# Linear attention feeding a GELU feed-forward block: k and v laid out nine tokens to a partition, numerators in four 64x64 tiles of TensorE

## The chip, the cores and the metric

The kernel runs on one core of one Trainium2 chip. The metric is the device time of one execution in microseconds (us); each time given is a median of several executions. Engines are named as the profile names them: PE is TensorE's matmul stream and PEld its weight loads, DVE is VectorE, ACT is ScalarE, POOL is GpSimd, SP is SyncE, whose queue issues the loads and the DMA transposes.

## The reference, cut to what matters

For each of 8 batches and 8 heads, with 576 tokens of 64 elements, a linear attention is computed, and its result goes through a feed-forward block with a tanh GELU.

```python
phi = lambda x: np.where(x > 0, x, np.exp(x) - 1.0) + 1.0
q_p, k_p = phi(q), phi(k)                        # (8, 8, 576, 64)
kv  = np.einsum('bhsd,bhse->bhde', k_p, v)       # 64 x 64 for each head
z   = np.sum(k_p, axis=2)
num = np.einsum('bhsd,bhde->bhse', q_p, kv)
den = np.einsum('bhsd,bhd->bhs', q_p, z)[..., None] + 1e-06
x   = (num / den).transpose(0, 2, 1, 3).reshape(4608, 512)
h   = x @ w_in                                   # 512 -> 2048
out = gelu_tanh(h) @ w_out                       # 2048 -> 512
```

The sum over tokens in kv does not care which token lies on which partition, so k and v may be laid out in any way that both share. The order of q's tokens decides the rows of the output.

## The kernel before: the parts that matter

The kernel treats 512 tokens of each batch as one group (four chunks of 128 tokens), and the last 64 tokens of all batches, two batches side by side, as a ninth group. `iteration(j)` runs the feed-forward block of group j in 32 slots: 16 of `h` (four matmuls each, then a GELU on ACT) and 16 of `o` (four matmuls each). Work for the next batches is put between slots by `at(j, slot, ...)`; `run` executes it after the slot's matmuls.

```python
def h_mm(h_ps, xt, m, ts=slice(0, MAIN)):          # one slot of h: 4 matmuls of 128x512
    for c in range(KM):
        nc.tensor.matmul(h_ps[:, ts], lhsT=w_in_sb[:, c, P*m : P*(m+1)], rhs=xt[:, c, ts], ...)
```

In batches 0 and 1, k and v lie nine tokens to a partition (one partition holds a run of nine tokens of one head, a partition half for each of two heads of a pair), and kv is made by 72 matmuls in 64x64 tiles. From batch 2 on, k and v lie four tokens to a partition for 512 tokens, and the last 64 come in separate tiles (`kr`, `vr`) shared by two batches, with the other batch's half of `vr` zero; kv is made by 40 matmuls that use 128 rows and 64 columns of the array.

```python
def kv_paired(b, ii, kv_of):                       # batches 0 and 1: 64x64 tiles
    for j in range(J):                             # J = 9
        for s in range(2):
            for a in range(2):
                r, u = slice(HP*a, HP*(a+1)), 2*ii + s
                nc.tensor.matmul(kv_of(a, ii)[HP*s : HP*(s+1)],
                                 lhsT=kp[r, j, u, :], rhs=vp[r, j, u, :], ...)

def kv_main(b, i, kv_ps):                          # batches 2 to 7: 128x64 tiles
    for c in range(C + 1):                         # 4 chunks and the rest
        for s in range(2):
            h = 2*i + s
            nc.tensor.matmul(kv_ps[HP*s : HP*(s+1), i, :],
                             lhsT=kp[:, c, h, :] if c < C else kr[:, 0, h, :],
                             rhs=vp[:, c, h, :] if c < C else vr[:, h, :], ...)
```

The numerator and denominator of a chunk come from four matmuls, one for each pair of heads, against a block-diagonal 128x130 tile `kvbd` (the off-diagonal blocks are zero; the 65th column of a block is z). DVE divides.

```python
def nab_mm(qt_c, kvbd, ns, rows=slice(0, P)):
    for i in range(NP):                            # NP = 4 pairs of heads
        nc.tensor.matmul(ns[i//2][rows, 2*E*(i%2) : 2*E*(i%2+1)],
                         lhsT=qt_c[:, i, rows], rhs=kvbd[:, i, :], ...)   # E = 65
...
def nab_evac(n_ps, paired):
    nc.vector.reciprocal(r, n_v[:, :, :, D])
    nc.vector.tensor_tensor(x_view(x, paired), n_v[:, :, :, 0:D], r[...].to_broadcast(...), op=ALU.mult)
```

The schedule of the later batches:

```python
def plan_prepare(b, s_linear, s_exp):
    ...
    at(j, s, linear, "q"); at(j, s + 1, linear, "k"); at(j, s + 2, casts)
    j, s = s_exp
    at(j, s, exps_all)          # q, then k, then kr
    at(j, s + 2, least_q)       # phi of q, and its four DMA transposes to qt
    at(j, s + 4, least_k)

def plan_attention(b, j, s_kv, s_n):
    ...
    at(j, s_kv, kv)
    for c in range(C):
        at(j, s_n[c], n, c)     # nab, then a DMA transpose of x to xt
...
for b in range(4, B):
    plan_prepare(b, (b - 2, 13), (b - 2, 15))
    if b > 4:
        at(b - 3, 23, load_batch, b)
for m in range(1, 4):
    at(2*m - 1, 18, load_rest, "qr", q, m)
    plan_rest(m, 2*m, 15, 22, (4, 5, 7)[m - 1])
for b in range(3, B):
    plan_attention(b, b - 1, 2, (4, 6, 8, 10))
```

PSUM's eight banks are six of a rotating pool (`bank`: h, o, kv, and n where it is made in single banks) and one pair (`pair_of_banks`) for n.

Of the kernel before, what the change touches and what calls it, by code (L numbers as in the profile page):

```python
# [15 lines left out]
def kernel(  # L16
# [34 lines left out]
    prest = ctx.enter_context(tc.tile_pool(name="prest", bufs=1))  # L51
# [31 lines left out]
    PAIRED = (0, 1)  # L83

    def ld_tile(name, b):
        shape = [P, NP, J * D] if b in PAIRED and name != "q" else [P, H, C * D]
        ld[name, b] = pld.tile(shape, FP32, name=name + "_x", tag="ld")
# [10 lines left out]
    def load_main(name, src, b):  # L98
        ld_tile(name, b)
        nc.sync.dma_start(  # L100
            out=ld[name, b],
            in_=src[b, :, 0:MAIN, :].rearrange("h (p c) d -> p h (c d)", c=C),
        )

    def load_rest(name, src, m):
        t = (pqr if name == "qr" else prest).tile([P, H, D], FP32, name=name)
        ld[name, m] = t
        for s in range(2):
            r = t[REST * s : REST * (s + 1)]
            rows = src[2 * m + s, :, MAIN:S, :]  # L110
            if name == "qr" and m == 0:
                for a in range(2):
                    nc.sync.dma_start(
                        out=r[:, NP * a : NP * (a + 1), :],
                        in_=rows.rearrange("(u a) p d -> p a u d", a=2)[:, a],
                    )
            else:
                nc.sync.dma_start(out=r, in_=rows.rearrange("h p d -> p h d"))

    def load_batch(b):  # L120
        load_main("q", q, b)
        load_main("k", k, b)
        if b % 2 == 0:
            load_rest("kr", k, b // 2)
            load_rest("vr", v, b // 2)
        load_main("v", v, b)
# [43 lines left out]
    load_main("q", q, 3)  # L170
    load_main("k", k, 3)
# [8 lines left out]
    vrs = [const.tile([P, H, E], BF16, name=f"vr{s}") for s in range(2)]  # L180
    kvbds = [const.tile([P, NP, 2 * E], BF16, name=f"kvbd{i}") for i in range(4)]
    for i in range(2):
        nc.gpsimd.memset(vps[i][:, :, D:E], 1.0)
        nc.gpsimd.memset(kvbds[i], 0.0)
    for s in range(2):
        nc.gpsimd.memset(kvbds[2 + s], 0.0)
        nc.gpsimd.memset(vrs[s], 0.0)
        nc.gpsimd.memset(vrs[s][REST * s : REST * (s + 1), :, D:E], 1.0)
# [3 lines left out]

    def vp_main(b):
        return vps[b % 2][:, 0 : C * H].rearrange("p (c h) e -> p c h e", h=H)
# [5 lines left out]
    def by_chunk(t, hs):  # L200
        return t[:, :, hs, :].rearrange("p c h d -> p h c d")
# [5 lines left out]
    def exp_of(name, b, hs=None):  # L207
        x = ld[name, b]
        hs = hs or slice(0, x.shape[1])
        if (name, b) not in exps:  # L210
            exps[name, b] = pe.tile([P, x.shape[2] // D, x.shape[1], D], BF16, name=name + "_e")
        nc.scalar.activation(  # L212
            by_chunk(exps[name, b], hs),
            x[:, hs].rearrange("p h (c d) -> p h c d", d=D),
            AF.Exp,
        )

    def linear_of(name, b, hs=None):
        x = ld[name, b]
        hs = hs or slice(0, x.shape[1])  # L220
        if (name, b) not in phi:
            phi_tiles(name, b)
        nc.vector.tensor_scalar(  # L223
            by_chunk(phi[name, b], hs),
            x[:, hs].rearrange("p h (c d) -> p h c d", d=D),
            1.0,
            1.0,
            op0=ALU.add,
            op1=ALU.max,
        )  # L230
# [14 lines left out]

    def cast_v(b, fn):
        fn(
            out=vp_main(b)[:, :, :, 0:D].rearrange("p c h d -> p h c d"),
            in_=ld["v", b].rearrange("p h (c d) -> p h c d", d=D),
        )  # L250

    def cast_vr(m):
        for s in range(2):
            r = slice(REST * s, REST * (s + 1))
            nc.vector.tensor_copy(out=vrs[s][r, :, 0:D], in_=ld["vr", m][r])
# [16 lines left out]
    def kv_main(b, i, kv_ps):  # L272
        kp, vp = phi["k", b], vp_main(b)
        kr, vr = phi["kr", b // 2], vrs[b % 2]
        for c in range(C + 1):
            for s in range(2):
                h = 2 * i + s
                nc.tensor.matmul(  # L278
                    kv_ps[HP * s : HP * (s + 1), i, :],
                    lhsT=kp[:, c, h, :] if c < C else kr[:, 0, h, :],  # L280
                    rhs=vp[:, c, h, :] if c < C else vr[:, h, :],
                    start=(c == 0),
                    stop=(c == C),
                    skip_group_check=True,
                )

    def kv_evac(b, blocks, src, fn):
        for s in range(2):
            r = slice(HP * s, HP * (s + 1))
            fn(out=kvbds[b % 4][r, blocks, E * s : E * (s + 1)], in_=src[r])  # L290

    def nab_mm(qt_c, kvbd, ns, rows=slice(0, P)):
        for i in range(NP):
            nc.tensor.matmul(  # L294
                ns[i // 2][rows, 2 * E * (i % 2) : 2 * E * (i % 2 + 1)],
                lhsT=qt_c[:, i, rows],
# [4 lines left out]
    def x_view(x, paired):  # L301
        return x.rearrange("p (u a d) -> p a u d" if paired else "p (a u d) -> p a u d", a=2, d=D)

    def nab_evac(n_ps, paired):
        n_v = n_ps[:, :, 0 : 4 * E].rearrange("p a (u e) -> p a u e", e=E)
        r = psm.tile([P, 2, NP], FP32, name="r")
        nc.vector.reciprocal(r, n_v[:, :, :, D])  # L307
        x = px.tile([P, d_model], BF16, name="x")
        nc.vector.tensor_tensor(  # L309
            x_view(x, paired),  # L310
            n_v[:, :, :, 0:D],
            r[:, :, :, None].to_broadcast([P, 2, NP, D]),
            op=ALU.mult,
        )
        return x

    def nab(qt_c, b):
        n_ps = pair_of_banks("n_ps")
        nab_mm(qt_c, kvbds[b % 4], [n_ps[:, a] for a in range(2)])
        return nab_evac(n_ps, b in PAIRED)  # L320

    def nab_in_banks(qt_c, b):
        ns = [bank("n_ps", [P, 4 * E]) for _ in range(2)]
        nab_mm(qt_c, kvbds[b % 4], ns)
        x = px.tile([P, d_model], BF16, name="x")
        for a in range(2):
            n_v = ns[a].rearrange("p (u e) -> p u e", e=E)
            r = psm.tile([P, NP], FP32, name="r1")
            nc.vector.reciprocal(r, n_v[:, :, D])
            nc.vector.tensor_tensor(  # L330
                x_view(x, b in PAIRED)[:, a],
                n_v[:, :, 0:D],
                r[:, :, None].to_broadcast([P, NP, D]),
                op=ALU.mult,
            )
        return x
# [184 lines left out]
    def plan_prepare(b, s_linear, s_exp):  # L521
        rest = b % 2 == 0

        def linear(n):
            linear_of(n, b)
            if rest and n == "k":
                linear_of("kr", b // 2)

        def casts():
            cast_v(b, nc.vector.tensor_copy)  # L530
            if rest:
                cast_vr(b // 2)

        def exps_all():
            for n in "qk":
                exp_of(n, b)
            if rest:
                exp_of("kr", b // 2)

        def least_q():  # L540
            least_of("q", b)
            qts[b] = pt.tile([P, C, NP, P], BF16, name="qt")
            for c in range(C):
                nc.sync.dma_start_transpose(
                    out=qts[b][:, c],
                    in_=phi["q", b][:, c].rearrange("p h d -> p (h d)"),
                )

        def least_k():
            least_of("k", b)  # L550
            if rest:
                least_of("kr", b // 2)

        j, s = s_linear
        at(j, s, linear, "q")
        at(j, s + 1, linear, "k")
# [3 lines left out]
        at(j, s + 2, least_q)  # L560
        at(j, s + 4, least_k)

    def plan_attention(b, j, s_kv, s_n):
        def kv():
            if j == 1:
                kv_ps = pair_of_banks("kv_ps")[:, 0, 0 : NP * E].rearrange("p (i e) -> p i e", e=E)
            else:
                kv_ps = bank("kv_ps", [P, NP, E])
            for i in range(NP):
                kv_main(b, i, kv_ps)  # L570
            kv_evac(b, slice(0, NP), kv_ps, nc.vector.tensor_copy)

        def n(c):
            x = nab(qts[b][:, c], b)
            if c == 0:
                xts[b] = pt.tile([P, NP, MAIN], BF16, name="xt")
            nc.sync.dma_start_transpose(out=xt_chunk(b, c), in_=x)

        at(j, s_kv, kv)
        for c in range(C):  # L580
            at(j, s_n[c], n, c)

    def plan_rest(m, j, s_exp, s_least, j_n):
        box = {}

        def least():
            linear_of("qr", m)
            least_of("qr", m)
            box["qt"] = psm.tile([P, NP, P], BF16, name="qtr")
# [164 lines left out]
```

## Time and profile before

| | |
|---|---|
| time | 287.52 us, median of 3 (287.31 to 287.77) |
| profiled span | 285.5 us, TensorE clock granted 0.998 |
| PE busy | 278.1 us (97%), 1864 matmuls |
| PEld busy | 136.5 us (48%) |
| ACT busy | 163.8 us (57%) |
| DVE busy | 107.7 us (38%) |
| POOL busy | 20.5 us (7%) |
| DMA | 53.76 MB, mean 188 GB/s |

Busy time of an engine is the time in which one of its instructions ran, and shares are of the span. Matmuls overlap in their pipeline, so PE's busy time says that it always had one under way, not that each ran at its best spacing; what a group of matmuls costs is read from when the next group starts. The chain of waits follows the work back from the last instruction, and what stands in it set the end.

### The profile page before, as it was taken

Reading aid. Unit: us, or ns where it says so; the run is one execution under the profiler, and the core shown is the slowest. Engines: PE = TensorE matmul, PEld = TensorE weight load, DVE = VectorE, ACT = ScalarE, POOL = GpSimd, SP = SyncE. Lnnn points to the kernel's source line nnn. Section 1 sums busy time; section 2 is a strip of 40 time slices with the busy share of each in tenths; the row PEclk is TensorE's granted clock in tenths of the full one; section 3 lists DMA queues with packets and bytes.
Section 4 is the critical chain, followed back from the end, with each engine's and each line's share of the span. In section 5 each row is a group of like instructions: output and inputs, shape, how many; then the busy total and the mean of one; then the engine's idle time right before and its main releaser. Section 6 shows DMA issues by size and latency. Waiting matters only on the chain.

```text
span 285.5 us, 4570 instructions
## 1 busy us (share of the span) xinstructions
PE 278.1 (97%) x1864; PEld 136.5 (48%) x1864; DVE 107.7 (38%) x182; ACT 163.8 (57%) x226; POOL 20.5 (7%) x26
## 2 busy tenths in 40 slices
PE   8789999999999999999999999999999999999995
PEld 3464455445454445544554455444544444444444
DVE  3840468534855473543246614640412010000001
ACT  4866865795966935683458635763572275027400
POOL 6066250000000000000000000000000000000000
PEclk9999999999999999999999999999999999999999
DMA  7999999966979948936899489435141230120022
GB/s 247 410 406 397 410 400 270 365 229 195 146 231 327 252 141 230 340 75 149 227 276 216 115 219 363 79 103 156 37 39 45 87 53 0 53 86 10 0 74 74
DMA packets 71539, 53.76 MB, mean 188 GB/s; under 512 B 42080, under 2 KB 62944, under 8 KB 71520
## 3 DMA queue, kind: packets, MB, share of 16 engines
q1 hardware_dynamic: 68736, 44.58, 55.8%
q10 hardware_dynamic: 2784, 8.91, 8.7%
q8 instruction: 14, 0.23, 0.3%
q14 instruction: 5, 0.04, 0.0%
HBM read 36.70 MB, written 9.44 MB: 162 GB/s over the span
## 4 chain that ended last, share of the span: by engine, by line
PE 93%; DMA 3%; DVE 1%; SPq 1%; issue 0%; ACTq 0%; ACT 0%; DVEq 0%
PE h_ps L349 44%; PE o_ps L650 43%; PE n_ps L294 3%; DMA v_x<-in_v_dram 3%; PE kv_ps L278 1%; PE t_ps L341 1%; SPq L91 1%; PE kv_ps L263 0%; SPq L96 0%; PE t_ps L474 0%; DVE x L330 0%; DVE vp L241 0%; DVE x L309 0%; PE w_ps L385 0%; ACTq L616 0%
## 5 line engine op out<-in xcount | busy, mean ns | idle before, releaser
L650 PE MATMUL o_ps<-w_out_sb,g 128*128 128x512 bf16 (+2 forms) x608 | 127.5, 368 | 0.0
L349 PE MATMUL h_ps<-xt,w_in_sb 128*128 128x512 bf16 (+1 forms) x552 | 117.6, 363 | 0.0
L359 ACT ACTIVATE g<-h_ps 128x512 bf16<-128x512 f32 x144 | 85.0, 598 | 46.2 <-PE h_ps L349 45.2
L650 PEld LDWEIGHTS <-g 128*128 128x128 bf16 x608 | 57.8, 98 | 64.4
L349 PEld LDWEIGHTS <-w_in_sb 128*128 128x128 bf16 x616 | 56.4, 97 | 59.7 <-issue 0.6
L611 ACT COPY o_sb<-o_ps 128x512 f32<-128x512 f32 (+2 forms) x20 | 11.1, 561 | 60.6 <-PE o_ps L650 53.5
L611 DVE COPY o_sb<-o_ps 128x512 f32<-128x512 f32 (+1 forms) x18 | 12.0, 666 | 69.9 <-PE o_ps L650 69.9
L307 DVE RECIPROCAL r<-n_ps 128x8 f32<-128x8 f32 x33 | 6.8, 207 | 49.0 <-PE n_ps L294 48.9
L309 DVE TENSOR_TENSOR x<-n_ps,r 128x512 bf16<-128x512 f32 x33 | 22.8, 691 | 1.1
L212 ACT ACTIVATE q_e<-q_x 128x2048 bf16<-128x2048 f32 (+1 forms) x9 | 15.5, 1721 | 2.8 <-DMA q_x<-in_q_dram 2.7
L212 ACT ACTIVATE k_e<-k_x 128x2048 bf16<-128x2048 f32 (+2 forms) x9 | 15.8, 1755 | 0.8 <-DMA k_x<-in_k_dram 0.8
L223 DVE TENSOR_SCALAR q_p<-q_x 128x2048 bf16<-128x2048 f32 (+1 forms) x9 | 9.9, 1100 | 14.2 <-DMA q_x<-in_q_dram 14.2
L236 DVE TENSOR_TENSOR q_p<-q_p,q_e 128x2048 bf16<-128x2048 bf16 (+1 forms) x9 | 9.9, 1105 | 13.4 <-ACT q_e L212 13.3
L349 PE MATMUL h_ps<-xt_rest,w_in_sb 128*128 128x512 bf16 x64 | 14.0, 379 | 0.0
L294 PEld LDWEIGHTS <-qt 128*128 128x128 bf16 x128 | 9.7, 98 | 6.9 <-DVE x L309 0.4
L294 PE MATMUL n_ps<-kvbd,qt 128*128 128x130 bf16 x128 | 12.5, 221 | 0.0
L223 DVE TENSOR_SCALAR k_p<-k_x 128x2048 bf16<-128x2048 f32 (+2 forms) x9 | 10.2, 1132 | 5.4 <-DMA k_x<-in_k_dram 5.4
L236 DVE TENSOR_TENSOR k_p<-k_p,k_e 128x2048 bf16<-128x2048 bf16 (+2 forms) x9 | 11.0, 1227 | 0.8 <-ACT k_e L212 0.7
L290 DVE CAST kvbd<-kv_ps 64x260 bf16<-64x260 f32 (+2 forms) x18 | 6.6, 365 | 10.7 <-PE kv_ps L278 8.2
L385 PE MATMUL w_ps<-warm 128*128 128x512 bf16 x32 | 9.3, 444 | 1.2 <-DVE warm L177 1.2
L376 ACT ACT_TABLE_LOAD x8 | 10.3, 1283 | 0.1
L212 ACT ACT_TABLE_LOAD x8 | 10.3, 1283 | 0.1
(49 smaller groups left out, 96.6 us busy)
## 6 DMA issues: line engine op xcount, KB each, us to landing
out_dram<-o_sb ACTq DMA_DIRECT2D x16, 512.0 KB, 3.1
q_x<-in_q_dram SPq DMA_DIRECT2D x6, 1024.0 KB, 7.5
k_x<-in_k_dram SPq DMA_DIRECT2D x6, 1024.0 KB, 11.3
v_x<-in_v_dram SPq DMA_DIRECT2D x6, 1024.0 KB, 7.5
w_st<-in_moe_w_in_dram SPq DMA_DIRECT2D x4, 1024.0 KB, 14.5
w_st<-in_moe_w_out_dram SPq DMA_DIRECT2D x4, 1024.0 KB, 13.6
q_x<-in_q_dram SPq DMA_DIRECT2D x4, 512.0 KB, 8.5
k_x<-in_k_dram SPq DMA_DIRECT2D x2, 576.0 KB, 5.6
```

The costliest lines, as they stand in the source:

```text
L212: nc.scalar.activation(by_chunk(exps[name, b], hs), x[:, hs].rearrange("p h (c d) -> p h c d", d=D), AF.Exp,)
L223: nc.vector.tensor_scalar(by_chunk(phi[name, b], hs), x[:, hs].rearrange("p h (c d) -> p h c d", d=D), 1.0, 1.0, op0=ALU.add, op1=ALU.max,)
L236: nc.vector.tensor_tensor(p, p, e, op=ALU.min)
L294: nc.tensor.matmul(ns[i // 2][rows, 2 * E * (i % 2) : 2 * E * (i % 2 + 1)], lhsT=qt_c[:, i, rows], rhs=kvbd[:, i, :], skip_group_check=True,)
L307: nc.vector.reciprocal(r, n_v[:, :, :, D])
L309: nc.vector.tensor_tensor(x_view(x, paired), n_v[:, :, :, 0:D], r[:, :, :, None].to_broadcast([P, 2, NP, D]), op=ALU.mult,)
L349: nc.tensor.matmul(h_ps[:, ts], lhsT=w_in_sb[:, c, P * m : P * (m + 1)], rhs=xt[:, c, ts], start=(c == 0), stop=(c == KM - 1), skip_group_ ...
L359: nc.scalar.activation(g[:, m, :], h_ps, AF.Gelu_apprx_tanh)
L376: nc.scalar.preload_act_table_set("gelu_apprx_tanh_and_others")
L385: nc.tensor.matmul(w_ps, lhsT=warm[:, 0:P], rhs=warm)
L611: (nc.scalar.copy if on_scalar else nc.vector.tensor_copy)(dst, src)
L650: nc.tensor.matmul(o_ps, lhsT=g[:, m, P * t : P * (t + 1)], rhs=w_out_sb[:, m, fs], start=(m == 0), stop=(m == MM - 1),)
```

## The change

It makes one form out of two. In all batches k and v come in nine tokens to a partition, so the separate tiles for the last 64 tokens of k and v, their loads, their maps and the zeroed `vr` tiles go. The numerators of batches 3 to 7, and of all leftover tokens of q, are made in four 64x64 tiles of the array from a plain `kv` tile (128x65 for a pair of heads) instead of the block-diagonal one. Two chunks are made in one slot, at two slots of a group (5 and 21) instead of four (4, 6, 8, 10) and one for kv (2); the next batch's kv shares the later slot. Loads of batches 5 to 7 are issued at slot 6 of a group instead of 23. In batches 4 to 7 the map of k runs ahead of that of q. The aim is to enter the small-tile modes of TensorE less often and to use all of the array in them.

The core of the diff, with cuts:

```diff
-    def load_main(name, src, b):
+    def load_q(b):
+        ...
+    def load_all_pairs(name, src, b):
         ld_tile(name, b)
-        nc.sync.dma_start(
-            out=ld[name, b],
-            in_=src[b, :, 0:MAIN, :].rearrange("h (p c) d -> p h (c d)", c=C),
-        )
+        load_pairs(name, src, b)
...
-    def kv_main(b, i, kv_ps):
-        ...
+    def kv_of_head(b, s, i):
+        r = slice(HP * s, HP * (s + 1))
+        return kvs[b % 4][r, i, :] if b > 2 else kvbds[b][r, i, E * s : E * (s + 1)]
+
+    def n_quads(qt_c, bs, ns):
+        for i in range(NP):
+            for t in range(2):
+                for s in range(2):
+                    c = slice(HP * t, HP * (t + 1))
+                    nc.tensor.matmul(
+                        ns[s][c, E * i : E * (i + 1)],
+                        lhsT=qt_c[HP * s : HP * (s + 1), i, c],
+                        rhs=kv_of_head(bs[t], s, i),
+                        skip_group_check=True,
+                    )
...
+        order = "qk" if b < 4 else "kq"
...
-        at(j, s + 2, least_q)
-        at(j, s + 4, least_k)
+        if b < 4:
+            at(j, s + 2, least_q, b)
+            at(j, s + 4, least_of, "k", b)
+        else:
+            at(j, s + 2, least_of, "k", b)
...
+    def plan_attention(b, m_rest):
+        j = b - 1
+        def pair_of_chunks(c):
+            in_banks = nab_quads_in_banks(qts[b][:, c + 1], (b, b))
+            in_pair = nab_quads(qts[b][:, c], (b, b))
+            return (c + 1, in_banks), (c, in_pair)
+        def early():
+            chunks = pair_of_chunks(0)
+            if m_rest is not None:
+                rest = nab_quads_in_banks(rest_qt[m], (2 * m, 2 * m + 1))
+            ...
+        def late():
+            chunks = pair_of_chunks(2)
+            if b + 1 < B:
+                kv_ps = [bank("kv_ps", [P, 2, E]) for _ in range(2)]
+                for ii in range(2):
+                    kv_paired(b + 1, ii, lambda a, ii: kv_ps[a][:, ii, :])
+            for c, x_of in chunks:
+                transposed_x(b, c, x_of())
+            if b + 1 < B:
+                ...                                # kv copied to SBUF on DVE
+                least_q(b + 1)
+        at(j, 5, early)
+        at(j, 21, late)
...
-    plan_attention(2, 1, 16, (18, 20, 22, 24))
+    plan_third()                                   # kv_in_pair(2) at (1, 16), four n as before
...
+    at(2, 2, kv_in_pair, 3)
     for b in range(4, B):
         plan_prepare(b, (b - 2, 13), (b - 2, 15))
-        if b > 4:
-            at(b - 3, 23, load_batch, b)
...
-    for b in range(3, B):
-        plan_attention(b, b - 1, 2, (4, 6, 8, 10))
+    for b in range(3, B):
+        plan_attention(b, {4: 0, 5: 1, 6: 2, 7: 3}.get(b))
+    for b in range(5, B):
+        at(b - 3, 6, load_batch, b)
```

Batches 0 and 1 keep their code. Batch 2 keeps the block-diagonal numerators, with its kv now made by the 72 matmuls of `kv_paired`.

## The prediction, made before the changed kernel ran

> **What bounds the kernel now.** I read the busy shares first, then the chain of waits, then the chain in order of time, because only the last says what a small group of matmuls costs. The page's first and fourth parts:
>
> ```profile
> PE 278.1 (97%) x1864; PEld 136.5 (48%) x1864; DVE 107.7 (38%) x182; ACT 163.8 (57%) x226; POOL 20.5 (7%) x26
> ...
> PE 93%; DMA 3%; DVE 1%; SPq 1%; issue 0%; ACTq 0%; ACT 0%; DVEq 0%
> ```
>
> PE is the bound. The chain leaves PE only in the first 16 us and in the last microsecond; the 3% of DMA is the first loads, which the change keeps. So only time taken out of PE's stream after 60 us counts. The chain in order of time (start, length, what, number of matmuls), first in batch 1, then around two later groups:
>
> ```profile
> 41.45 0.71 PE kv_ps L263 x72
> 42.16 0.97 PE o_ps L650 x4
> ...
> 43.60 0.86 PE o_ps L650 x4
> ...
> 80.92 0.76 PE kv_ps L278 x40
> 81.68 1.83 PE h_ps L349 x8
> 83.51 0.23 PE n_ps L294 x4
> 83.74 1.73 PE h_ps L349 x8
> ...
> 110.34 0.37 PE n_ps L294 x8
> 110.71 0.64 PE kv_ps L278 x40
> 111.35 1.83 PE h_ps L349 x8
> 113.18 0.23 PE n_ps L294 x4
> 113.41 1.73 PE h_ps L349 x8
> ```
>
> The reader is to see two things. Eight full matmuls take 1.73 us (216 ns each), but 1.83 us after a kv, so leaving a small-tile mode costs 0.1 us that the chain books on the matmuls behind. And nothing stands between the pieces: in steady groups PE waits for nobody. The extra time of a group over its 128 full matmuls is therefore the sum of its small pieces.
>
> [...] Read record by record, the first small-tile matmul starts 93 ns later than a full one would have, and the first full one starts about 125 ns after the last small one and is followed by one spaced 10 ns too wide. [...]
>
> **The change, part by part.** First the unit costs, all from the trace before.
>
> - A chunk of numerators, 4 matmuls of 128x130: 0.236 us from where the next full matmul could have started, without a mode change.
> - kv in 40 matmuls of 128x64: 0.76 + 0.10 = 0.86 us. With the 8 leftover numerators ahead in the same mode: 0.37 + 0.64 + 0.10 = 1.11 us. The last leftovers alone (group 7): 0.46 + 0.01 = 0.47 us.
> - kv in 72 matmuls of 64x64, that is 18 rounds of four tiles: 0.71 + (0.97 - 0.86) = 0.82 us. Its rounds start on average 33 ns apart (0.563 us from the first to the eighteenth), so an episode of R rounds costs about 0.22 + 0.033 R us. This is an estimate from one episode. The 0.22 is entering and leaving.
>
> A chunk in 64x64 tiles is 16 matmuls, 4 rounds. So, after the change, two chunks alone are 8 rounds, 0.48 us; two chunks and the leftovers 12 rounds, 0.62 us; two chunks and a kv 26 rounds, 1.08 us.
>
> | group j | before | after |
> |---|---|---|
> | 1 (batch 2) | 0.86 + 4 x 0.236 = 1.80 | 0.82 + 0.94 = 1.76 |
> | 2 | 1.80 | kv of batch 3 alone 0.82, early 0.48, late 1.08 = 2.38 |
> | 3, 4, 5 | 1.11 + 0.94 = 2.05 each | 0.62 + 1.08 = 1.70 each |
> | 6 | 1.80 | 0.62 + 0.48 = 1.10 |
> | 7 | 0.47 | 0 |
> | sum | 12.0 | 10.3 |
>
> The sum is **1.7 us less**. It is a small number because the numerators of one chunk fall only from 0.236 to 0.13 us, kv is hardly cheaper in 72 small matmuls than in 40 larger ones, and each group of batches 3 to 6 now pays for a small-tile mode twice where it paid once. Group 2 gets slower because it carries two kv.
>
> Now what moves off PE, and whether it comes back as a wait. The late slot's kv needs the map of k of the same group. I place it on the trace before, group 5's start of o at 153.28:
>
> ```profile
> 153.93 1.28 ACT L212 ACT_TABLE_LOAD   x1
> 154.90 1.23 DVE L247 CAST vp<-v_x 128x2048 bf16<-128x2048 f32 x1 [2.37 <-DMA v_x<-in_v_dram]
> 155.23 1.91 ACT L212 ACTIVATE q_e<-q_x 128x2048 bf16<-128x2048 f32 x1
> ...
> 157.17 1.23 DVE L236 TENSOR_TENSOR q_p<-q_p,q_e 128x2048 bf16<-128x2048 bf16 x1 [0.25 <-ACT q_e L212]
> ```
>
> After the change k goes first, with 2304 elements to a partition: its exp takes 2.11 us (batch 1's row of that shape), so 155.23 to 157.34, and the minimum on DVE 1.23 x 2304/2048 = 1.38 us, to 158.75. PE reaches slot 21's end at 153.28 + 6 x 0.864 = 158.46, enters the mode (0.09), does 8 rounds (0.27) and wants k at 158.82. That is 0.07 us of slack: none, within my error. I charge an expected wait of 0.06 us in four groups, **0.25 us**.
>
> The other deadlines have room. DVE, free at 158.75, copies one output tile (0.69), divides two chunks (1.3 in single banks, 0.9 in the pair) and is done at 161.7; the two DMA transposes need some 1.4 us of SP each and land 2.6 to 3.7 us after issue, so by about 166, while the next group starts at 153.28 + 13.82 + 1.08 = 168.2. The transposes of the next q follow, by about 171, and are wanted at slot 5 of the next group, 173.4. PSUM: with the leftovers, the early slot takes four extra banks of six; the GELU of slot 3 must be done by the end of slot 5, and GELUs run about 0.9 us behind their matmuls, so it is.
>
> Off PE, DVE gains about 0.37 us for each pair of chunks and each leftover tile divided in single banks (two reciprocals and two multiplies, 1.27, against 0.90), loses the maps of kr and the casts of vr (0.42 + 0.42 + 0.87 in three batches); ACT loses three exps of 0.61 us and gains 0.2 us for each k. All of it is beside PE. The loads lose 12 transfers of 128 KB in 256-byte rows, and come earlier; the one visible DMA wait there, the 2.37 us ahead of the v cast, ends no wait of PE.
>
> 287.52 - 1.74 + 0.25 = **286.0 us**.
>
> **The rivals.** (1) *kv waits for k in the late slot.* The slack above is nil. If ACT or DVE runs 0.4 us later than I placed them, four groups lose 0.4 us each, the gain is gone, and the time is about 287.4. The order k before q speaks for an author who saw that wait and cured it. (2) *The new numerators run slower than batch 1's kv.* They load a new weight tile for every 65 columns, as kv does, but a late slot holds 104 matmuls in a row where the trace shows 72 at most, and in the last rounds of those 72 the starts within a round already spread from 3 to 8 ns. At 60 ns a round instead of 33, the 96 rounds of numerators (20 chunks and 4 leftover tiles, 4 rounds each) would cost 2.6 us more: about 288.6. (3) *The transposes land late*, since two chunks now come only 10 slots before the next group; it would show as a wait of h at a group's head, at most 1 us in five groups, 289 or more. The margin of 2 us speaks against it. (4) *The gain is larger*, since earlier and longer loads help: nothing in the steady chain waits for a load, so I give this nothing beyond 0.3 us.
>
> **Range and chances.** The account gives 285.8 without any wait and 287.4 if rival 1 is full; numerators at 27 ns a round (65 columns at the rate of 216 ns for 512) would take 0.6 us off the former, 285.2. I take 285.2 to 287.1 for 8 in 10. A gain of over 2% needs 5.75 us, nearly half of all small pieces (12 us): 1 in 100. Over 2% slower needs a stall of more than 1 us in most groups: 2 in 100.
>
> **What would show each step.** In the chain of the changed kernel: late pieces of about 0.97 us for x104 followed by 0.11 us more on the next four matmuls; early pieces of 0.37 to 0.5 us; a period of 29.3 us in groups 3 to 5 (27.64 + 1.70) against 29.67 now; group 2 longer by 0.6 us; group 7 at 27.6 us. A wait of PE's kv for DVE's k minimum is rival 1; wider rounds without a wait are rival 2; a wait of h for a DMA at a group's head is rival 3. I am wrong if tiles that do not accumulate behave differently from batch 1's, or if DVE reaches its deadlines later than placed.

## The result, and the profile after

The changed kernel takes **297.0 us** (median of 6, 295.58 to 298.27), against 287.56 for the kernel before beside it: 1.0327 times as long, with a 95% interval of 1.0288 to 1.0366. I had predicted 286.0, with 287.1 as the upper end. The profiled run of the changed kernel is the longest of its six, with a span of 296.5 us against 285.5.

The busy shares and the chain by engine, first and fourth parts of its page:

```profile
PE 280.2 (95%) x2294; PEld 137.1 (46%) x2328; DVE 105.0 (35%) x197; ACT 161.2 (54%) x221; POOL 17.9 (6%) x21
...
PE 82%; DMA 11%; DVE 3%; issue 2%; SPq 1%; ACT 0%; ACTq 0%; DVEq 0%
```

PE's busy time hardly moved (278.1 to 280.2), which by itself would say that nothing had happened. The chain says otherwise: DMA had 3% of it, all in the first microseconds, and now has 11%. The waits of PE (who waits, for whom, us in total, times, longest) name two that were not there. Before, all of them; then the first three after:

```profile
PE kv_ps L263 <- DVE vp L241: 1.5, 2, 1.1
PE w_ps L385 <- DVE warm L177: 1.2, 1, 1.2
PE t_ps L341 <- DVE x L309: 0.8, 1, 0.8
PE t_ps L341 <- DVE x L330: 0.5, 1, 0.5
```
```profile
PE h_ps L348 <- DMA xt<-x: 4.4, 2, 3.6
PE kv_ps L236 <- DVE vp L225: 1.9, 2, 1.2
PE kv_ps L236 <- DVE k_p L220: 1.4, 1, 1.4
```

Of the three, the middle one belongs to the first two batches, whose code did not change (1.5 us before); the first and the last are new. The chain in order of time (start, length, what) shows them in place:

```profile
88.30 0.38 PE n_ps L270 x32
88.68 1.85 PE h_ps L348 x4
...
91.09 10.61 DMA v_x<-in_v_dram
...
103.00 1.36 DVE k_p L220
...
104.41 0.78 PE kv_ps L236 x72
...
105.34 2.05 PE o_ps L672 x9
107.39 9.98 DMA xt<-x
...
117.50 4.42 PE h_ps L348 x10
```

In group 2 the late slot's kv of batch 4 starts at 104.41, late because DVE's minimum for k stands behind the cast of v, and v lands at 101.70. Then a transpose of x issued at 107.39 takes 9.98 us to land, and h of group 3 starts at 117.50. Its first ten matmuls take 4.42 us; at full clock ten take 2.16. PE had idled 3.6 us, and its matmuls run at half clock until 123.5, for 6 us. SyncE's queue shows what was issued ahead of that transpose, batch 5's three loads:

```profile
98.36 0.54 SPq L98 DMA_DIRECT2D q_x<-in_q_dram  x1
99.02 2.53 SPq L89 DMA_DIRECT2D k_x<-in_k_dram  x1
101.66 0.45 SPq L89 DMA_DIRECT2D v_x<-in_v_dram  x1
106.08 5.15 SPq L569 DMA_TRANSPOSE xt<-x  x2
```

The last of these loads lands at 115.0, the two transposes at 116.6 and 117.4.

The loss of 11.0 us in span, read from the starts of the groups in both chains:

| stretch | lost in it |
|---|---|
| until group 1 begins (48.5 us before, 51.6 after) | 3.1 |
| group 1 and the wait at the head of group 2 (78.25, 82.08) | 0.7 |
| group 2 and the wait at the head of group 3 (107.75, 117.50) | 5.9 |
| group 3, in its beginning at half clock | 2.8 |
| groups 4 to 8 | -1.5 |

The first row is the surprise: the code and the transfers of that stretch are unchanged. The windows of both profiles (stretch, length, busy time of each engine, granted clock, DMA share, GB/s) show slower transfers. Before, then after:

```profile
0.00:40.00 40.00, 36.06 (x307) 19.37 (x308) 18.96 (x33) 29.27 (x38) 18.26 (x25) 1.00 0.99 378
```
```profile
0.00:40.00 40.00, 35.34 (x277) 19.71 (x281) 16.48 (x31) 26.41 (x35) 14.88 (x19) 0.91 0.99 357
```

The DMA engines are full in both (0.99), but move 357 GB/s instead of 378. Read packet by packet between 5 and 40 us, the 2048-byte packets have a median of 87 ns instead of 84, those of 2304 bytes 98 instead of 93. The clock of 0.91 is something else: one fall to half, from 14.2 to 21.1 us, after a stretch (10 to 14 us) in which PE was busy for 2.01 of 4 us. Two of the later profiles have this fall too, and o of their first group starts at 33.7 to 34.0 us; six others with equally slow loads do not have it, and there o starts at 31.4 to 31.8.

### The profile page after: what moved, and what is told of

The parts are those of the page before. It is cut to its first block, busy times and chain, and to the rows that moved or that the text cites. A ratio compares the mean times of both kernels' runs of the same rounds, so it can differ in the third digit from the quotient of the medians.

```text
span 296.5 us, 5430 instructions
## 1 busy us (share of the span) xinstructions
PE 280.2 (95%) x2294; PEld 137.1 (46%) x2328; DVE 105.0 (35%) x197; ACT 161.2 (54%) x221; POOL 17.9 (6%) x21
## 4 chain that ended last, share of the span: by engine, by line
PE 82%; DMA 11%; DVE 3%; issue 2%; SPq 1%; ACT 0%; ACTq 0%; DVEq 0%
PE h_ps L348 41%; PE o_ps L672 35%; DMA v_x<-in_v_dram 7%; DMA xt<-x 4%; PE kv_ps L236 2%; PE n_ps L270 1%; PE n_ps L252 1%; PE t_ps L340 1%; DVE x L283 1%; SPq L89 1%; DVE k_p L220 0%; DVE q_p L214 0%; DVE q_p L220 0%; SPq L94 0%; PE t_ps L473 0%
## 5 line engine op out<-in xcount | busy, mean ns | idle before, releaser
L348 PE MATMUL h_ps<-xt,w_in_sb 128*128 128x512 bf16 (+2 forms) x537 | 117.3, 373 | 5.4 <-DMA xt<-x 4.4
L348 PEld LDWEIGHTS <-w_in_sb 128*128 128x128 bf16 x616 | 59.2, 101 | 71.2 <-issue 9.4
L283 DVE TENSOR_TENSOR x<-n_ps,r 128x256 bf16<-128x256 f32 (+1 forms) x53 | 27.6, 520 | 1.8
L282 DVE RECIPROCAL r<-n_ps 128x4 f32<-128x4 f32 (+1 forms) x53 | 9.8, 184 | 49.1 <-PE n_ps L270 43.2
L220 DVE TENSOR_TENSOR k_p<-k_p,k_e 128x2304 bf16<-128x2304 bf16 (+1 forms) x9 | 11.0, 1223 | 20.1 <-ACT k_e L206 20.1
L206 ACT ACTIVATE k_e<-k_x 128x2304 bf16<-128x2304 f32 (+1 forms) x9 | 17.1, 1905 | 1.0 <-DMA k_x<-in_k_dram 0.9
L214 DVE TENSOR_SCALAR k_p<-k_x 128x2304 bf16<-128x2304 f32 (+1 forms) x9 | 11.0, 1220 | 12.5 <-DMA k_x<-in_k_dram 12.5
L225 DVE CAST vp<-v_x 128x2304 bf16<-128x2304 f32 (+1 forms) x9 | 10.4, 1159 | 0.9 <-DMA v_x<-in_v_dram 0.9
L236 PE MATMUL kv_ps<-vp,k_p 64*64 64x65 bf16 x576 | 6.5, 194 | 3.3 <-DVE vp L225 1.9
L129 POOL CAST w_in_sb<-w_st 128x2048 bf16<-128x2048 f32 (+1 forms) x5 | 7.7, 1551 | 16.1 <-DMA w_st<-in_moe_w_in_dram 16.1
```

Of the source, the lines that this page charges most:

```text
L206: nc.scalar.activation(o, i, AF.Exp)
L214: nc.vector.tensor_scalar(o, i, 1.0, 1.0, op0=ALU.add, op1=ALU.max)
L220: nc.vector.tensor_tensor(p, p, e, op=ALU.min)
L225: fn(out=vp_paired(b)[:, :, us, 0:D].rearrange("p j u d -> p u j d"), in_=ld["v", b][:, us].rearrange("p u (j d) -> p u j d", d=D),)
L236: nc.tensor.matmul(kv_of(a, ii)[HP * s : HP * (s + 1)], lhsT=kp[r, j, u, :], rhs=vp[r, j, u, :], start=(j == 0), stop=(j == J - 1), skip_g ...
L282: nc.vector.reciprocal(r, n_v[heads + (D,)])
```

## The experiments

### Is the slow start the kernel's? And the two loads moved

Two kernels were run unchanged, to see whether the slow start is the chip's.

> The kernel before, unchanged, profiled beside the changed one on one chip. Open question: in the changed kernel's profile the first loads, which are the same transfers, run about 5% slower (385 against 405 GB/s between 5 and 40 us) and o of the first group starts at 34.0 us against 31.1. If that is a property of the chip or of the moment, this profile shows o starting near 34 us too and the loads near 385 GB/s, with a time near 290 us. If it is a property of the changed kernel, this one shows 31.1 us and 405 GB/s again, with 287.5 us.

> The changed kernel, unchanged, on the same chip as the others of this set. If the slow first loads belong to the kernel: o of the first group starts near 34 us and the time is 295.5 to 298.5 us. If they belong to the chip of the earlier profile: o starts near 31 us, and the time is 293 to 295 us, as the stalls of groups 1 to 3 (0.95, 1.7 and 3.7 us, and about 3 us of lowered clock after the last) stay.

Measured: 287.75 us for the kernel before, with 376 GB/s in the first 40 us; 295.12 us for the changed one, with 357 GB/s. The slow start **belongs to the kernel**: o of the first group starts at 33.7 us again. The time lies just under the range that I had given for this case.

Then loads were moved. First batch 5's alone:

```diff
-        at(b - 3, 6, load_batch, b)
+        at(b - 3, 23 if b == 5 else 6, load_batch, b)
```

> The changed kernel with batch 5's loads alone issued at slot 23 of group 2, as before, instead of slot 6. Theory A (batch 5's loads follow batch 4's on the DMA rings and the late transposes of x of batch 3 queue behind them): the 3.7 us wait of h for xt at the head of group 3 goes, and with it the lowered clock behind it (about 3 us); time about 290 to 291 us; the 1.7 us wait of kv in group 2's late slot stays. Rival (the transposes are late for another reason, the late slot itself being too late): the wait at the head of group 3 shrinks by less than half and the time stays over 294 us.

Measured: 298.72 us, 1.0367 [1.0311, 1.0422] times the kernel before, so **no gain**. But the wait had not stayed: the chain has none at the head of group 3, and this at the head of group 4.

```profile
135.11 5.14 PE o_ps L672 x23
140.28 0.66 DVE o_sb L633
140.93 7.73 DMA xt<-x
...
148.79 4.43 PE h_ps L348 x10
```

A transpose of x issued at 140.93 lands 7.7 us later, and half clock follows again. The collision had moved by one group: now batch 6's loads, at slot 6 of group 3, came right behind batch 5's, at slot 23 of group 2. The expected gain failed, and so did the rival's wait at the head of group 3. What held of theory A is that the late slot's transposes land only after the loads issued ahead of them, of which the last landed here at 144.0, and that these land late where two batches of loads come in a row.

The next adds to it batch 4's loads two slots sooner:

```diff
-    at(1, 29, load_batch, 4)
+    at(1, 27, load_batch, 4)
```

> As the kernel with batch 5's loads at slot 23, and batch 4's loads issued at slot 27 of group 1 instead of 29, ahead of the transpose of the leftover q. Theory B (kv of batch 4 is now wanted at slot 21 of group 2, one group earlier than before, and v of batch 4 lands too late for it because its issue stands in SP's queue behind the wait for the leftover q): v lands 2 us earlier, the 1.7 us wait of kv in group 2 goes or falls below 0.3 us; time 1.4 to 1.8 us under the kernel with batch 5's loads alone moved. Rival (the loads are limited by the rings, not by their issue): v lands within 0.7 us of where it did and the time falls by less than 0.7 us.

Measured: 296.79 us, 1.0315 [1.0276, 1.0354], 1.9 us under the one before it, though the times of either kernel spread over about 3 us. What decides is the trace: v of batch 4 lands at 100.4 us instead of 102.0, and the wait of kv for k in group 2 fell from 2.2 to 0.6 us, theory B's direction, if not quite its size; the wait at the head of group 4 stayed (5.6 us).

### The layout of SBUF

Why would unchanged loads slow down? The change takes constants away, so all tiles allocated behind them move. In the built programs the loads' tiles begin at byte 70400 of a partition before and at 69408 after: the former is a multiple of 256, the latter lies 32 past one. Adding an unused constant moves all of these tiles and does nothing else:

```diff
     kvs = [const.tile([P, NP, E], BF16, name=f"kv{i}") for i in range(4)]
+    const.tile([P, 16], BF16, name="pad")          # 32 bytes; later 96 and 992
```

> The changed kernel with an unused tile of 32 bytes to a partition behind its constants, and nothing else: the loads' SBUF destinations then begin at a multiple of 64 bytes, as in the kernel before, instead of 32 bytes past one (the changed constants are 992 bytes shorter to a partition). Theory C (loads into rows that start 32 bytes off run some 5% slower): 2048-byte packets take 84 ns again instead of 88, o of the first group starts at 31.1 us instead of 33.8, and the waits on loads in groups 1 to 3 shrink; time 286.5 to 290 us. Rival (the layout has nothing to do with it; the new loads slow the queue): packets stay at 88 ns and the time stays at 295 to 299 us.

Measured: 294.81 us, 1.0292 [1.0235, 1.035], 360 GB/s, packets of 2048 bytes still at 88 ns. With 32 bytes of padding the tiles lie at a multiple of 64, but 64 past one of 256. The theory as I had put it, a boundary of 64 bytes, **fell**.

> The kernel before with the same unused 32 bytes behind its constants: its loads now begin 32 bytes past a multiple of 64. Theory C: packets of 2048 bytes take 88 ns instead of 84, o of the first group starts near 34 us instead of 31.1, and the time is about 290.5 us (290 to 291.5), as the rest of this schedule has slack for its loads. Rival: 84 ns and 287.5 us.

Measured: 289.9 us, 1.0094 [1.0079, 1.0109]. The kernel before, with nothing changed but an unused 32 bytes, loses 2.7 us, and its packets of 2048 bytes go from 84 to 88 ns. Its windows:

```profile
0.00:40.00 40.00, 35.13 (x300) 18.68 (x301) 16.94 (x32) 28.44 (x37) 16.93 (x24) 1.00 0.99 358
```

So the address is the cause of the slow start, and only the size of the boundary was wrong. Of the 3.1 us lost before group 1, 2.3 are this (group 1 begins at 50.9 us here); the rest goes with the early fall of the clock: group 1 begins at 51.4 to 51.6 us in the three profiles that have it, at 50.8 to 51.2 in the six that do not. I had expected o of the first group near 34 us, which was the clock's doing and not the address's. It starts at 31.5, and 1.8 us of the loss come in that o, where PE waits 1.1 us for w_out.

The loads were also put back to where they had been, the leftover q's with them:

```diff
-        at(b - 3, 6, load_batch, b)
+        at(b - 3, 23, load_batch, b)
-    at(3, 6, load_rest, 2)
-    at(4, 6, load_rest, 3)
+    at(3, 18, load_rest, 2)
+    at(4, 18, load_rest, 3)
```

> The changed kernel with the loads of batches 5 to 7 back at slot 23 and the leftover q's at slot 18, as before. The kernel with batch 5's loads alone moved had its 5.3 us wait at the head of group 4 instead of 3. Theory A (a load issued at slot 6 right behind the one of the group before delays the late transposes): now no group head waits over 1 us, and the time is 290 to 292.5 us: 3 us of slower start and about 2.5 us of kv waiting for batch 4's v in group 2 stay over 286.4 us, which the measured small pieces give without any wait. Rival (the late slot is too late for its transposes in any case): waits of some us appear at the heads of groups 3, 4 and 5, and the time stays over 295 us.

Measured: 290.97 us, 1.0147 [1.0108, 1.0185]. No head of a group waits over 0.7 us, and kv waits 1.8 us for k in group 2. Theory A holds in this form: **loads at slot 6 cost the transposes**. The leftover q's loads moved in the same edit, and their part of it was not measured alone.

> Both: 32 bytes of padding, and the loads of batches 5 to 7 back at slot 23. If theories A and C cover the loss, the time is 286 to 288 us, with at most 1.5 us of kv waiting for v in group 2. If a third cause stands, it is over 289 us.

Measured: 290.11 us, 1.0102 [1.0087, 1.0117]. As the 32 bytes did not cure the packets (88 ns), this could not be the test of both causes that I meant; it repeats the one before within 0.9 us.

### The right boundary, and both causes together

> The changed kernel with 96 unused bytes: the loads' tiles begin on a multiple of 128 but not of 256 bytes. If 256 bytes is the boundary that matters, packets of 2048 bytes stay at 88 ns and the time near 295 us; if 128 is enough, 84 ns.

Measured: 88 ns, 296.29 us. At 128 bytes past the boundary it is as slow as at 32 or 64.

> The changed kernel with 992 unused bytes to a partition behind its constants, so that all later tiles lie exactly where they lay before relative to a 256-byte boundary (the kernel before has its loads' tiles at a multiple of 256 bytes, the changed one 32 past; the 32 bytes of padding tried first left them 64 past, and nothing changed). Theory C', loads are slow unless their rows begin on a 256-byte boundary: 2048-byte packets take 84 ns, o of the first group starts at 31.1 us. What stays is the crowding of loads in groups 2 and 3, smaller by the earlier start: time 289 to 293 us. Rival (not the address): packets stay at 88 ns and the time at 295 us.

Measured: 84 ns, and the start is the old one, with group 1 at 48.6 us. The time is 293.84 us, 1.0244 [1.0201, 1.0287], over the 289 to 293 that I had expected: with the loads still at slot 6, the two waits in groups 2 and 3 stay, and they did not shrink with the earlier start as I had thought. Its waits of PE:

```profile
PE h_ps L349 <- DMA xt<-x: 5.4, 2, 5.0
PE kv_ps L237 <- DVE k_p L221: 2.1, 1, 2.1
```

> 992 bytes of padding, and the loads of batches 5 to 7 back at slot 23. Both causes taken away: 2048-byte packets at 84 ns, no wait of a group's head over 0.3 us, kv of batch 4 waiting up to 1 us for v in group 2. The small pieces as measured (0.63 early, 1.21 late) give 286.4 us without waits; so 286.4 to 287.6 us. If a third cause stands, it is over 288.5 us.

Measured: 287.26 us over 12 runs, 0.9997 [0.9983, 1.0012]. **Both causes taken away, the loss is gone.** Loads at slot 23 are worth 6.6 us here (293.84 less 287.26), and the layout 3.7 us (290.97 less 287.26). kv still waits 0.7 us for k in group 2.

> As the one before, and batch 4's loads issued at slot 27 of group 1 instead of 29, ahead of the transpose of the leftover q. The wait of kv in group 2 goes: 286.2 to 286.8 us, 0.3 to 0.8 us under the one before, and under the kernel before the change by 0.7 to 1.3 us. Rival: the earlier loads delay that transpose or the q of batch 3 and a new wait takes the place of the old; then no gain over the one before.

Measured: 286.60 us, 0.9973 [0.9961, 0.9984] times the kernel before: 0.6 us under the kernel before, where I had expected 0.7 to 1.3, and 0.7 under the one before it. No wait of PE is left that the kernel before does not have. Its waits of PE, complete:

```profile
PE t_ps L341 <- DVE x L284: 1.3, 2, 0.8
PE w_ps L385 <- DVE warm L169: 1.2, 1, 1.2
PE o_ps L673 <- issue: 0.8, 5, 0.2
PE kv_ps L237 <- DVE vp L226: 0.4, 1, 0.4
PE w_ps L385 <- issue: 0.2, 1, 0.2
PE h_ps L349 <- issue: 0.2, 1, 0.2
```

All of those for DVE lie in the first 16 us, in the code of batch 0. The waits put down to issue, 0.2 us each, stand where a matmul's record is missing from the trace.

## Why the prediction was wrong, by its own steps

**The pieces on PE held.** The steady groups came out nearly as summed. From the chain of the last kernel above, where nothing waits:

```profile
113.64 0.53 PE n_ps L271 x48
...
128.09 0.38 PE n_ps L271 x32
128.47 0.73 PE kv_ps L237 x72
...
143.13 0.53 PE n_ps L271 x48
```

From early slot to early slot is 29.49 us (143.13 less 113.64); I had 29.3. Two chunks alone cost 0.48 us (predicted 0.48), with the leftovers 0.63 (0.62), kv of 72 matmuls alone 0.81 (0.82). Only the late slot was mis-sized: 1.21 us instead of 1.08, taken from a trace whose records are complete there. Read record by record, PE starts its first kv matmul 0.15 us after the last numerator, where a round mostly follows the last within 0.02 to 0.03 us. The four kv matmuls behind the gap last 214 ns each, like the four that open a small-tile episode, and not 190 like the rest. I don't know why; no run tried to take this gap away. Four such slots take 0.5 us off the 1.7 us: the pieces sum to 10.9 us against 12.0 before, 1.1 us less. The last kernel's profiled span, of its shortest run, is 1.2 us below that of the kernel before, and its median 0.6 us.

**"The loads ... come earlier ... ends no wait of PE" is the step that failed**, together with the margin of 2 us that I gave rival 3. I had taken a transpose's time to land, 2.6 to 3.7 us, from medians, and medians mix two cases. In the trace before, too, 5 of the 24 transposes of x took 5.2 to 6.3 us, all issued while a batch's loads were landing; the last of each group's four, with the loads nearly done, took 2.4 to 2.7. That cost nothing, as those five were made in slots 4 to 6 and wanted only at the next group's head. With 992 bytes of padding and the loads at slot 23 the early slot's transposes take up to 10.8 us, and nobody waits, while those of the late slot, from group 2 on, land in 2.3 to 5.6. Loads at slot 6 turn this round: they stand ahead of the late slot's transposes, which are wanted 10 slots later. The first of them, batch 5's, were issued while batch 4's were still landing (until 101.7 us), so they ended late, at 115.0, and the transposes took 10 us. One batch alone was just in time: in group 3 of the same run the late transposes land by 149.6, and h of group 4 starts at 149.9 without a wait. The whole group 3 wait, with its half clock behind it, is this; the two kernels with 992 bytes of padding size the early loads at 6.6 us (293.84 against 287.26).

**kv of batch 4 wanted 13 slots sooner** (slot 21 of group 2 instead of slot 2 of group 3). I followed k through ACT and DVE to the late slot and found no slack, but on the profile of a later group, and for k alone. In group 2, v of batch 4 is the last to land, as before, and the cast of v stands ahead of k's minimum in DVE's order. Rival 1 named the right wait (kv for k's minimum) with the wrong cause (ACT and DVE; it was the load) and in four groups instead of one. In groups 3 to 5, where I had charged 0.06 us each, kv does not wait for k.

**"The first loads, which the change keeps"** was true of the instructions and wrong of their addresses. Nothing in my working looked at where the tiles lie. It cost 2.7 us in the kernel before when provoked alone, and 3.7 us in the changed one.

**Rivals 2 and 4** did not happen. That the new numerators run at the rate of batch 1's kv, as the sum has it, was an assumption, and the runs bore it out: eight rounds of numerators take 0.25 us from the first start to the eighth, as do the first eight rounds of batch 1's kv, and 18 rounds of kv behind them take 0.56, as in batch 1. The longer rows of k and v gave no visible gain.

## What to carry to other kernels

In the changed kernel a transpose of x took from 2.4 to 10.6 us to land, the longest with a batch's loads ahead of it, so before moving a load, list the transposes and stores that will be issued behind it and when they are wanted. Here two late ones behind batch 5's three loads (1024, 1152 and 1152 KB) left PE idle for 3.6 us, and the 6 us of matmuls that followed ran at half clock. When a change takes or adds a constant, compare the base addresses of the tiles that loads write, and pad them back: here 32 bytes decided 1% of the time. And check each input of work that is brought forward, in the first group where it runs, and not one input in a settled group.

## What the runs showed of the hardware that I had not expected

With the loads' tiles beginning at byte 70400 of a partition, a multiple of 256, the first 40 us moved 376 to 379 GB/s; with the tiles 32, 64 or 128 bytes past such a multiple, 357 to 360 GB/s, with packets some 5% longer (48 against 46 ns at 1024 bytes, 87 to 88 against 84 at 2048, 98 to 99 against 93 at 2304). As 70400 is no multiple of 512, 256 is the only power of two that divides this address and none of the others. Further addresses were not tried, and what makes up the 5% stays open.

PE idle for 3.6 us in the middle of dense work came back at half clock for 6 us: its matmuls started 427 ns apart instead of 216. After the 1.4 us wait in the same run it did not. Of the waits inside the dense work of all profiles here, the seven of 3.0 to 5.6 us were each followed by half clock, and those up to 2.2 us by none. The early fall, at 14.2 us, came without any wait over 1.3 us, and in the kernel with batches 4's and 5's loads moved the same two waits for vp (1.2 and 0.7 us) went by without it.
